# Scores and state @ w_in as groups of eight 64x32 matmuls, and softmax weights taken from VectorE block transposes

## The chip, the cores and the metric

The kernel runs on one core of one Trainium2 chip. The metric is the device time of one execution in microseconds (us). A core has a matrix engine (TensorE, called PE in the profile; its weight loads are the rows PEld), VectorE (DVE), ScalarE (ACT), GpSimd (POOL) and SyncE (SP), which here only issues DMAs. Each engine works through its own instructions in order and waits for the others by semaphores.

## What is computed

The reference is a cross attention between tokens `x` and a small recurrent state, followed by a feed-forward block. There are 8 batches, 8 heads, 512 tokens of 64 numbers per head, and 32 states per head; the feed-forward block goes from 512 to 2048 and back to 512. All is float32; the two weight matrices arrive as float64.

```python
# x: (8, 8, 512, 64)   state: (8, 8, 32, 64)
scores  = scale * x @ state^T          # 512 x 32 per head
a       = softmax(scores)              # over the 32 states
xread   = a @ state
scores2 = scale * state @ x^T          # 32 x 512 per head
a2      = softmax(scores2)             # over the 512 tokens
sread   = a2 @ x
y = concat([xread, sread])             # (8, 544 tokens, 512)
h = y @ w_in                           # 512 -> 2048
out = (h * sigmoid(1.702 * h)) @ w_out # 2048 -> 512
```

`scores2` is the transpose of `scores`; only the axis of the softmax differs.

## The kernel before

`xread @ w_in` is taken as `a @ M` with M = `state @ w_in` per head, so that the first product of a batch contracts over 8 heads x 32 states = 256 rows instead of 512. The work of one batch has two stretches:

- **Up** (`up`, matmuls at line 301, tiles `h`): for each of 16 blocks of 128 columns, two matmuls of M against the transposed softmax weights `aT`; ScalarE takes the sigmoid (L303), VectorE multiplies (L305, tiles `g`).
- **Down** (`down`, L317, tiles `o`): for each of 4 row blocks, 16 matmuls against `w_out`, cut into 4 quarters, so 16 slots of 4 matmuls in all. After each quarter comes one slot of the *next* batch's attention, from the table in `att_slots`: the transpose of the state (`att_state`, L158), the transposes of x (`att_xT`, L172), the scores and their softmaxes, the transposes of the softmax weights, and `att_sread` (L263). In eight of the slots one piece of M (`att_M`, L231) is added behind.

Before the change, the state of each pair of heads stands in a block-diagonal tile `sbd` (128 rows: 2 heads x 64; 128 columns: 4 heads x 32, zero outside the pair's two blocks; written by four VectorE copies at L162). Three things are multiplied with it on the whole 128x128 array:

- `att_x_scores` (L183, two calls a batch, tiles `s` with 64 columns): scores with tokens on the partitions, for the softmax over states (L193 to L201 on VectorE, the exponential at L196 on ScalarE);
- `att_s_scores` (L211, two calls, tiles `s` with 512 columns): the same scores with states on the partitions, for the softmax over tokens (L213 to L220, the exponential at L217);
- `att_M` (L231, eight calls, two matmuls each), evacuated by one VectorE or ScalarE copy (L233).

`att_aT` (L243) then transposes the first softmax's weights on TensorE and ScalarE copies them out (L244); `att_eT` (L253) does so for the second.

Batch 0 has nothing to hide behind: its attention, the rounding of `w_in` from float64 words (`round_weight`, four VectorE instructions and two GpSimd ones per tile, L122 to L130) and M run first, and the rounding of `w_out` runs inside batch 0's up. The loads are issued by SP in program order: state and x of batch 0 (L88, L91), then `w_in` through three buffers (L103). The order on PE, ACT, POOL and SP is the program's; that on VectorE is set by the framework's scheduler. PSUM tiles of the attention come from a pool of four banks (`psA`).

Of the kernel before, what the change touches and what calls it, by code (L numbers as in the profile page):

```python
# [20 lines left out]
def kernel(  # L21
# [24 lines left out]
    HG = P // Ns             # heads of a group: their states fill the partitions  # L46
    NG = H // HG             # groups of heads
    NPR = H // 2             # pairs of heads: 2 * D rows
# [4 lines left out]
    NFC = DF // FC  # L53
    scale = float(1.0 / np.sqrt(D))
    eps = 1e-9
    assert (2 * D, HG * Ns, NPR * P, DM, NFC) == (P, P, DM, FC, SCH)

    out_b = out.rearrange("(b t) n -> b t n", b=B)
    x_v = x.rearrange("b h (c q) d -> b c q h d", q=P)
# [23 lines left out]
    xn, stn = {}, {}  # L83

    def load(b):
        stn[b] = apool.tile([P, NG, 2, D], FP32, tag="stn", name=f"stn_{b}")
        for k in range(2):
            nc.sync.dma_start(stn[b][:, :, k, :], st_v[b])  # L88
        xn[b] = xpool.tile([P, SCH, H, D], FP32, tag="xn", name=f"xn_{b}")
        for c in range(SCH):  # L90
            nc.sync.dma_start(xn[b][:, c], x_v[b, c])  # L91

    def x_pair(b, c, p):
        return xn[b][:, c, 2 * p : 2 * p + 2].rearrange("q h d -> q (h d)")
# [3 lines left out]
    w_in_words, w_out_words = moe_w_in.bitcast(I32), moe_w_out.bitcast(I32)  # L98
    raw = {}

    def load_weight(key, src):
        raw[key] = wpool.tile([P, 2 * FC], I32, tag="raw", name="raw_" + "_".join(map(str, key)), bufs=3)
        nc.sync.dma_start(raw[key], src)  # L103

    def load_w_in(c):
        for k in range(NPR):
            load_weight(("i", c, k), w_in_words[P * k : P * (k + 1), 2 * FC * c : 2 * FC * (c + 1)])

    def load_w_out(f):
        load_weight(("o", f), w_out_words[P * f : P * (f + 1)])  # L110
# [15 lines left out]
        # the fraction's upper 20 bits below the leading 1, then its lower 32 in one rounding  # L126
# [16 lines left out]
    # block-diagonal state^T of each pair of heads, zero elsewhere; each batch  # L143
    # rewrites the same blocks
    sbd = [konst.tile([P, NPR, P], FP32, name=f"sbd_{i}") for i in range(2)]
    for t in sbd:
        nc.gpsimd.memset(t, 0.0)
    # sread^T of all batches: [d of a pair, pair, batch, n]
    srT = konst.tile([P, NPR, B, Ns], FP32, name="srT")

# [1 line left out]
    A = {}  # L152

    def att_state(b):
        A[b] = {"sbd": sbd[b % 2]}
        ps = att_ps([P, NG, P], f"stT_{b}")
        for g in range(NG):
            nc.tensor.transpose(ps[:, g], stn[b][:, g].rearrange("p k d -> p (k d)"), ident)  # L158
        for j in range(HG):
            r = slice(D * (j % 2), D * (j % 2) + D)  # L160
            cols = slice(Ns * j, Ns * (j + 1))
            nc.vector.tensor_copy(  # L162
                sbd[b % 2][r].rearrange("p (g k) c -> p g k c", g=NG)[:, :, j // 2, cols],
                ps[r, :, cols],
            )

    def att_xT(b, p):
        if p == 0:
            A[b]["xT"] = apool.tile([P, NPR, S], FP32, tag="xT", name=f"xT_{b}", bufs=1)
        ps = att_ps([P, SCH, P], f"xT_{b}_{p}")  # L170
        for c in range(SCH):
            nc.tensor.transpose(ps[:, c], x_pair(b, c, p), ident)  # L172
        dst = A[b]["xT"][:, p]
        (nc.scalar.copy if p % 2 else nc.vector.tensor_copy)(dst, ps.rearrange("p c q -> p (c q)"))  # L174

    def att_x_scores(b, i):
        # softmax of the x tokens over the states, two chunks of tokens at a time
        a = A[b]
        ps = att_ps([P, 2, NPR, 2 * Ns], f"s1_{b}_{i}")
        for c in range(2):  # L180
            for p in range(NPR):
                o = 2 * Ns * (p % (HG // 2))
                nc.tensor.matmul(  # L183
                    ps[:, c, p],
                    a["xT"][:, p, P * (2 * i + c) : P * (2 * i + c + 1)],
                    a["sbd"][:, p, o : o + 2 * Ns],
                    start=True,
                    stop=True,
                )
        sv = ps.rearrange("p c k (j n) -> p (c k j) n", n=Ns)  # L190
        n = 2 * H
        mx = apool.tile([P, n], FP32, tag="mx", name=f"mx_{b}_{i}")
        nc.vector.reduce_max(out=mx, in_=sv, axis=AX.X)  # L193
        e = apool.tile([P, n, Ns], FP32, tag="e1", name=f"e1_{b}_{i}")
        nc.vector.tensor_tensor(out=e, in0=sv, in1=mx.to_broadcast((P, n, Ns)), op=ALU.subtract)  # L195
        nc.scalar.activation(out=e, in_=e, func=AF.Exp, scale=scale)  # L196
        sm = apool.tile([P, n], FP32, tag="sm", name=f"sm_{b}_{i}")
        nc.vector.reduce_sum(out=sm, in_=e, axis=AX.X)
        nc.vector.tensor_scalar(sm, sm, eps, None, ALU.add)
        nc.vector.reciprocal(out=sm, in_=sm)  # L200
        nc.vector.tensor_tensor(out=e, in0=e, in1=sm.to_broadcast((P, n, Ns)), op=ALU.mult)  # L201
        a["e1", i] = e

    def att_s_scores(b, g):
        # softmax of the states over the x tokens
        a = A[b]
        ps = att_ps([P, S], f"s2_{b}_{g}")
        k = NPR // NG
        for i in range(k):
            p = k * g + i  # L210
            nc.tensor.matmul(ps, a["sbd"][:, p], a["xT"][:, p], start=(i == 0), stop=(i == k - 1))  # L211
        mx = apool.tile([P, 1], FP32, tag="mx2", name=f"mx2_{b}_{g}")
        nc.vector.tensor_reduce(out=mx, in_=ps, axis=AX.X, op=ALU.max, negate=True)  # L213
        nc.vector.tensor_scalar(mx, mx, scale, None, ALU.mult)
        e = apool.tile([P, S], FP32, tag="e2", name=f"e2_{b}_{g}")
        sm = apool.tile([P, 1], FP32, tag="sm2", name=f"sm2_{b}_{g}")
        nc.scalar.activation(out=e, in_=ps, func=AF.Exp, bias=mx, scale=scale, accum_out=sm)  # L217
        nc.vector.tensor_scalar(sm, sm, eps, None, ALU.add)
        nc.vector.reciprocal(out=sm, in_=sm)
        nc.vector.tensor_scalar(e, e, sm, None, ALU.mult)  # L220
        a["e2", g] = e

    def att_M(b, c, g):
        a = A[b]
        if c == 0 and g == 0:
            a["M"] = mpool.tile([P, NG, DF], FP32, tag="M", name=f"M_{b}")
        ps = att_ps([P, FC], f"M_{b}_{c}_{g}")
        k = NPR // NG
        for i in range(k):
            p = k * g + i  # L230
            nc.tensor.matmul(ps, a["sbd"][:, p], w_in[c][:, p], start=(i == 0), stop=(i == k - 1))  # L231
        dst = a["M"][:, g, FC * c : FC * (c + 1)]
        (nc.scalar.copy if g else nc.vector.tensor_copy)(dst, ps)  # L233

    def att_aT(b, g):
        # x-token weights: [states of a group, tokens]
        a = A[b]
        if g == 0:
            a["aT"] = apool.tile([P, NG, S], FP32, tag="aT", name=f"aT_{b}", bufs=1)
        ps = att_ps([P, SCH, P], f"aT_{b}_{g}")  # L240
        for c in range(SCH):
            e = a["e1", c // 2].rearrange("p (c g j) n -> p c g (j n)", c=2, g=NG)
            nc.tensor.transpose(ps[:, c], e[:, c % 2, g], ident)  # L243
        nc.scalar.copy(a["aT"][:, g], ps.rearrange("p c q -> p (c q)"))  # L244

    def att_eT(b, g):
        # state weights: [tokens of a chunk, states of a group]
# [4 lines left out]
        for c in range(SCH):  # L252
            nc.tensor.transpose(ps[:, c], a["e2", g][:, P * c : P * (c + 1)], ident)  # L253
        nc.vector.tensor_copy(a["eT"][:, g], ps)  # L254

    def att_sread(b):
        a = A[b]
        ps = att_ps([P, NPR, 2 * Ns], f"sr_{b}")
        k = NPR // NG
        for p in range(NPR):  # L260
            o = 2 * Ns * (p % k)
# [138 lines left out]
```

## Time and profile before

| | |
|---|---|
| runs (us) | 1029.76, 1025.52, 1028.1; median 1028.1 |
| span of the profiled execution | 1027.2 us (the page gives no other time for it) |
| busy: PE, PEld | 965.7 us (94%), 476.3 us (46%) |
| busy: DVE, ACT, POOL | 318.7 us (31%), 181.5 us (18%), 74.0 us (7%) |
| granted TensorE clock, mean | 0.970 of full speed |

The span runs from the first to the last instruction. "Busy" of PE is the union of its matmul records, whose ends are modelled; a float32 matmul leaves two records, each with its own weight load, and a transpose leaves one. A mean duration per record is longer than the distance between the starts of two records, since one begins before the one ahead of it has ended. "Idle before" is time in which the engine stood still ahead of an instruction, with what released it.

### The profile page before, as it was taken

What the parts mean: (1) busy time and instruction counts of PE and PEld (TensorE: products, weight loads), DVE (VectorE), ACT (ScalarE), POOL (GpSimd) and SP (SyncE); (2) the same over time, 40 slices, a digit from 0 to 9 for tenths busy, and PEclk for the clock granted to TensorE, in tenths of its full rate; (3) what the DMA queues carried; (4) which work ended last, traced back from release to release, by engine and by line L of the source; (5) the groups of instructions that cost most, each with busy time, mean ns of one, the idle gap of its engine ahead of it and who ended that gap; (6) DMA issues with size and microseconds to landing.
All of it is one profiled execution on the core that took longest, in us unless ns stands there. A gap on an engine that the chain in (4) does not pass through costs nothing.

```text
span 1027.2 us, 7083 instructions
## 1 busy us (share of the span) xinstructions
PE 965.7 (94%) x2832; PEld 476.3 (46%) x2832; DVE 318.7 (31%) x592; ACT 181.5 (18%) x306; POOL 74.0 (7%) x106
## 2 busy tenths in 40 slices
PE   4757599999999999999999999999999999999996
PEld 3512145454545454544545454545454454444662
DVE  5798953123221313031312231132303131210110
ACT  0102112122111311131212111121113111310110
POOL 3244420000000000000000000000000000000000
PEclk9558999999999999999999999999999999999998
DMA  6255430020002000020002000200000000000000
GB/s 173 67 161 161 157 89 11 10 52 5 11 11 61 1 16 10 15 48 16 11 10 52 5 11 10 62 1 10 11 21 0 11 11 11 11 10 11 20 1 21
DMA packets 45377, 35.59 MB, mean 35 GB/s; under 512 B 39072, under 2 KB 39072, under 8 KB 45344
## 3 DMA queue, kind: packets, MB, share of 16 engines
q1 hardware_dynamic: 42240, 26.22, 9.5%
q0 software_dynamic: 3104, 8.92, 2.2%
q8 instruction: 22, 0.36, 0.1%
q14 instruction: 11, 0.09, 0.0%
HBM read 26.21 MB, written 8.91 MB: 34 GB/s over the span
## 4 chain that ended last, share of the span: by engine, by line
issue 68%; PE 19%; DVE 9%; POOL 2%; DMA 1%; SPq 0%; ACT 0%; POOLq 0%
PE o L317 9%; PE M L231 3%; PE h L301 3%; POOL out_dram L323 1%; PE sr L263 1%; DVE fr_o L128 1%; DVE w_in L130 1%; DVE g L305 1%; DVE fr_i L128 1%; DVE sc_o L125 1%; DVE w_out L130 1%; DVE w_out L129 1%; PE s L183 1%; PE s L211 1%; DVE sc_i L125 1%
## 5 line engine op out<-in xcount | busy, mean ns | idle before, releaser
L317 PE MATMUL o<-w_out,g 128*128 128x512 f32 x1024 | 456.8, 592 | 0.0
L317 PEld LDWEIGHTS o<-w_out,g 128*128 128x128 f32 x1024 | 191.3, 190 | 224.8 <-issue 224.8
L301 PE MATMUL h<-aT,M 128*128 128x512 f32 x512 | 225.6, 597 | 19.0 <-DVE g L305 19.0
L301 PEld LDWEIGHTS h<-aT,M 128*128 128x128 f32 x512 | 91.6, 190 | 148.2 <-DVE g L305 81.6
L231 PE MATMUL M<-w_in,sbd 128*128 128x512 f32 x256 | 133.2, 643 | 13.9 <-DVE w_in L130 13.8
L305 DVE TENSOR_TENSOR g<-h,e 128x512 f32<-128x512 f32 x128 | 88.3, 690 | 122.7 <-ACT e L303 122.7
L303 ACT ACTIVATE e<-h 128x512 f32<-128x512 f32 x128 | 76.4, 597 | 180.8 <-PE h L301 180.8
L231 PEld LDWEIGHTS M<-w_in,sbd 128*128 128x128 f32 x256 | 47.6, 202 | 68.5 <-issue 48.5
L323 POOL DMA_DIRECT2D out_dram<-osb x32 | 17.6, 550 | 807.2 <-ACT osb L322 807.2
L322 ACT COPY osb<-o 128x512 f32<-128x512 f32 x32 | 18.8, 586 | 224.5 <-PE o L317 126.4
L254 DVE COPY eT<-eT 128x512 f32<-128x512 f32 x16 | 11.1, 691 | 130.2 <-PE eT L253 130.1
L233 DVE COPY M<-M 128x512 f32<-128x512 f32 x32 | 22.0, 688 | 84.6 <-PE M L231 84.6
L233 ACT COPY M<-M 128x512 f32<-128x512 f32 x32 | 18.6, 582 | 95.1 <-PE M L231 95.0
L183 PEld LDWEIGHTS s<-sbd,xT 128*128 128x128 f32 x256 | 31.7, 196 | 6.7 <-issue 6.7
L263 PEld LDWEIGHTS sr<-eT,xn 128*128 128x128 f32 x256 | 33.0, 209 | 3.8 <-issue 3.8
L263 PE MATMUL sr<-eT,xn 128*128 128x64 f32 x256 | 32.8, 292 | 0.1
L183 PE MATMUL s<-sbd,xT 128*128 128x64 f32 x256 | 30.9, 276 | 0.0
L305 DVE TENSOR_TENSOR g_sr<-h_sr,e_sr 128x256 f32<-128x256 f32 x16 | 6.8, 425 | 75.3 <-ACT e_sr L303 75.3
L211 PE MATMUL s<-xT,sbd 128*128 128x512 f32 x64 | 30.0, 593 | 0.0
L174 ACT COPY xT<-xT 128x512 f32<-128x512 f32 x16 | 9.4, 586 | 107.7 <-PE xT L172 107.7
L196 ACT ACTIVATE e<-e 128x512 f32<-128x512 f32 x16 | 10.1, 630 | 101.3 <-DVE e L195 101.3
L301 PE MATMUL h_sr<-srT,w_in 128*128 128x256 f32 x128 | 27.8, 379 | 0.0
(56 smaller groups left out, 474.3 us busy)
## 6 DMA issues: line engine op xcount, KB each, us to landing
xn<-in_x_dram SPq DMA_DIRECT2D x32, 256.0 KB, 4.4
raw_i<-in_moe_w_in_dram SPq DMA_DIRECT2D x16, 512.0 KB, 4.0
raw_o<-in_moe_w_out_dram SPq DMA_DIRECT2D x16, 512.0 KB, 3.3
out_dram<-osb POOLq DMA_DIRECT2D x32, 256.0 KB, 2.3
stn<-in_state_dram SPq DMA_DIRECT2D x16, 64.0 KB, 2.2
out_dram<-osb_sr POOLq DMA_DIRECT2D x2, 256.0 KB, 7.0
```

The lines of the kernel that those rows point to most:

```text
L125: nc.vector.scalar_tensor_tensor(sc, hi, -0x80000000, sc, ALU.bitwise_and, ALU.bitwise_or)
L128: nc.vector.tensor_scalar(fr, hi, 0xFFFFF, 0x100000, ALU.bitwise_and, ALU.bitwise_or)
L183: nc.tensor.matmul(ps[:, c, p], a["xT"][:, p, P * (2 * i + c) : P * (2 * i + c + 1)], a["sbd"][:, p, o : o + 2 * Ns], start=True, stop=True,)
L211: nc.tensor.matmul(ps, a["sbd"][:, p], a["xT"][:, p], start=(i == 0), stop=(i == k - 1))
L231: nc.tensor.matmul(ps, a["sbd"][:, p], w_in[c][:, p], start=(i == 0), stop=(i == k - 1))
L233: (nc.scalar.copy if g else nc.vector.tensor_copy)(dst, ps)
L263: nc.tensor.matmul(ps[:, p], x_pair(b, c, p), a["eT"][:, p // k, c, o : o + 2 * Ns], start=(c == 0), stop=(c == SCH - 1),)
L301: nc.tensor.matmul(hps, lhs[i], rhs[i], start=(i == 0), stop=(i == n - 1))
L303: nc.scalar.activation(out=e, in_=hps, func=AF.Sigmoid, scale=1.702)
L305: nc.vector.tensor_tensor(out=gt, in0=hps, in1=e, op=ALU.mult)
L317: nc.tensor.matmul(ops, G[key][f][:, P * r : P * (r + 1)], w_out[f], start=(f == 0), stop=(f == NF - 1))
L323: nc.gpsimd.dma_start(dst, osb)
```

## The change

- `sbd` goes. The state of a batch is transposed once into one tile `stT` of 128x128: 64 rows for heads 0 to 3, 64 rows for heads 4 to 7, and 32 columns for each head of a half.
- A new `by_state` replaces the matmuls of the scores and of M. It issues eight matmuls of 64 rows by 32 columns with 512 moving columns, one for each head. Each addresses its own part of the array: rows by the half g, columns by the head j in the half. The halves write different PSUM banks.
- The scores are computed once, states on the partitions (`att_scores`, slot 6). The softmax over tokens reads them as before. The softmax over states reads a copy made by VectorE's 32x32 block transpose (L196), all 1024 values per partition at once (`att_x_softmax`), and a second block transpose (L221) gives `aT`. `att_aT` with its TensorE transposes and ScalarE copies goes.
- `att_M` is called four times a batch, in slots 8 to 11, instead of eight times in slots 2 to 9.
- Heads are paired as j and j + 4 instead of neighbours, so x is loaded in eight DMAs a batch instead of four, each `w_in` tile in two DMAs of 64 rows instead of one of 128, and the state in one instead of two.

The core of the diff (new line numbers: `by_state` matmul L179, transposes of x L169, `up` L284, `down` L300):

```diff
     def load(b):
-        stn[b] = apool.tile([P, NG, 2, D], FP32, tag="stn", name=f"stn_{b}")
-        for k in range(2):
-            nc.sync.dma_start(stn[b][:, :, k, :], st_v[b])
+        stn[b] = apool.tile([P, NG, D], FP32, tag="stn", name=f"stn_{b}")
+        nc.sync.dma_start(stn[b], st_v[b])
...
         for c in range(SCH):
-            nc.sync.dma_start(xn[b][:, c], x_v[b, c])
+            for g in range(NG):
+                nc.sync.dma_start(xn[b][:, c, :, g], x_v[b, c, g])
...
     def load_weight(key, src):
-        nc.sync.dma_start(raw[key], src)
+        for i in range(src.shape[0]):
+            n = P // src.shape[0]
+            nc.sync.dma_start(raw[key][n * i : n * (i + 1)], src[i])
...
+    def by_state(b, rhs, name):
+        ps = [att_ps([P, FC], f"{name}_{g}") for g in range(NG)]
+        for j in range(NPR):
+            for g in range(NG):
+                rows, st = slice(D * g, D * (g + 1)), slice(Ns * j, Ns * (j + 1))
+                nc.tensor.matmul(ps[g][st], A[b]["stT"][rows, st], rhs(rows, j), start=True, stop=True)
+        return ps
+
+    def att_scores(b):
+        a = A[b]
+        ps = by_state(b, lambda rows, j: a["xT"][rows, j], f"s_{b}")
...
+            nc.scalar.activation(out=e, in_=ps[g], func=AF.Exp, bias=mx, scale=scale, accum_out=sm)
+            nc.vector.transpose(t[:, g].rearrange("p i n -> p (i n)"), ps[g])
...
+    def att_x_softmax(b):
+        a = A[b]
+        n = NG * NB
+        t = a["e1"].rearrange("p g i n -> p (g i) n")
...
+        nc.vector.transpose(
+            a["aT"].rearrange("p g t -> p (g t)"), a["e1"].rearrange("p g i n -> p (g i n)")
+        )
...
-    def att_M(b, c, g):
+    def att_M(b, c):
...
-        for i in range(k):
-            p = k * g + i
-            nc.tensor.matmul(ps, a["sbd"][:, p], w_in[c][:, p], start=(i == 0), stop=(i == k - 1))
+        ps = by_state(b, lambda rows, j: w_in[c][rows, j], f"M_{b}_{c}")
...
-            at(5 + i, att_x_scores, b, i)
-        for g in range(NG):
-            at(7 + g, att_s_scores, b, g)
-        for g in range(NG):
-            at(10 + g, att_aT, b, g)
+        at(6, att_scores, b)
+        at(6, att_s_softmax, b)
+        at(7, att_x_softmax, b)
...
-            if ahead and 2 <= u < 2 + NFC * NG:
-                att_M(b + 1, *divmod(u - 2, NG))
+            if ahead and 8 <= u < 8 + NFC:
+                att_M(b + 1, u - 8)
```

What moves on the engines is seen in three places. In the rows, `o` is the output of down, `w_out` and `g` its operands; numbers behind a name are counters of tiles, and x8 stands for eight matmuls in a row.

**PE, down of batch 0, around slots 5 and 6.** Before, each quarter of down is followed by score matmuls and a piece of M:

```order
L317 MATMUL o_1_827<-w_out_106,g_7_626 128x512
L183 MATMUL s_1_0_846<-sbd_116,xT_788 128x64 x8
L231 MATMUL M_1_1_865<-w_in_96,sbd_116 128x512 x2
L317 MATMUL o_1_827<-w_out_107,g_8_644 128x512
...
L183 MATMUL s_1_1_873<-sbd_116,xT_788 128x64 x8
L231 MATMUL M_2_0_892<-w_in_97,sbd_116 128x512 x2
L317 MATMUL o_1_827<-w_out_111,g_12_716 128x512
```

and now by one group of eight small matmuls, first for the scores and from the ninth quarter on for M (the pair of rows comes four times in each group):

```order
L300 MATMUL o_1_813<-w_out_110,g_11_696 128x512
L179 MATMUL s_0_832<-xT_783,stT_777 32x512
L179 MATMUL s_1_833<-xT_783,stT_777 32x512
...
L300 MATMUL o_1_813<-w_out_111,g_12_714 128x512
...
L300 MATMUL o_2_881<-w_out_102,g_3_552 128x512
L179 MATMUL M_0_0_887<-w_in_95,stT_777 32x512
L179 MATMUL M_0_1_888<-w_in_95,stT_777 32x512
```

The score and M matmuls of the whole array have become five groups of eight, each between two matmuls of down.

**DVE, the same stretch.** Before, the softmax over states goes through two half-sized chains:

```order
L195 TENSOR_TENSOR e_1_0_857<-s_1_0_846,mx_0_855 128x512
L198 TENSOR_REDUCE sm_0_860<-e_1_0_857 128x16
L199 TENSOR_SCALAR sm_0_860<-sm_0_860 128x16
L200 RECIPROCAL sm_0_860<-sm_0_860 128x16
L201 TENSOR_TENSOR e_1_0_857<-e_1_0_857,sm_0_860 128x512
L193 TENSOR_REDUCE mx_1_882<-s_1_1_873 128x16
L195 TENSOR_TENSOR e_1_1_884<-s_1_1_873,mx_1_882 128x512
L233 COPY M_805<-M_2_0_892 128x512
```

and now through one chain of double width that begins and ends with block transposes:

```order
L196 STREAM_TRANSPOSE e_1_842<-s_1_833 128x512
...
L212 TENSOR_REDUCE mx_870<-e_1_842 128x32
...
L213 TENSOR_TENSOR e_1_842<-e_1_842,mx_870 128x1024
...
L231 COPY M_886<-M_0_0_887 128x512
L216 TENSOR_REDUCE sm_874<-e_1_842 128x32
L217 TENSOR_SCALAR sm_874<-sm_874 128x32
L218 RECIPROCAL sm_874<-sm_874 128x32
L219 TENSOR_TENSOR e_1_842<-e_1_842,sm_874 128x1024
L221 STREAM_TRANSPOSE aT_879<-e_1_842 128x1024
L231 COPY M_886<-M_1_0_903 128x512
```

The first copy of M stands ahead of the sum of the softmax, the second behind the whole chain.

**PE, the attention of batch 0, at the start of the program.** Before:

```order
L211 MATMUL s_0_1_254<-xT_179,sbd_115 128x512 x2
L243 MATMUL aT_0_267<-ident,e_0_0_215 128x128 x2
...
L253 MATMUL eT_0_280<-ident,e_0_0_248 128x128 x4
L253 MATMUL eT_1_286<-ident,e_0_1_260 128x128 x4
L263 MATMUL sr_292<-eT_279,xn_123 128x64 x16
L231 MATMUL M_0_0_312<-w_in_95,sbd_115 128x512 x2
L231 MATMUL M_0_1_316<-w_in_95,sbd_115 128x512 x2
```

and now:

```order
L179 MATMUL s_1_205<-xT_179,stT_177 32x512
L240 MATMUL eT_0_247<-ident,e_0_0_218 128x128 x4
L240 MATMUL eT_1_253<-ident,e_0_1_225 128x128 x4
L248 MATMUL sr_259<-eT_246,xn_118 128x64 x16
L179 MATMUL M_0_0_279<-w_in_95,stT_177 32x512
L179 MATMUL M_0_1_280<-w_in_95,stT_177 32x512
```

The transposes for `aT` no longer stand between the scores and those for `eT`, and both halves of M need all four tiles of a `w_in` chunk.

## Rows read from the trace of the kernel before

**Rows 1.** The page: busy tenths and granted clock in 40 slices of the span
```profile
PE   4757599999999999999999999999999999999996
...
DVE  5798953123221313031312231132303131210110
...
PEclk9558999999999999999999999999999999999998
```

**Rows 2.** Windows: length; busy us of PE, PEld, DVE, ACT, POOL; clock, DMA share, GB/s
```profile
244.26:354.70 110.44, 110.44 (x331) 53.86 (x330) 27.48 (x52) 21.76 (x36) 2.17 (x4) 1.00 0.08 21
...
0.00:133.81 133.81, 82.37 (x202) 38.52 (x203) 112.82 (x201) 18.93 (x31) 51.94 (x69) 0.80 0.47 146
```

**Rows 3.** Timeline of PE, one batch: start us, us, engine line op tiles xcount
```profile
247.69 0.38 PE L158 MATMUL stT<-ident,stn 128*128 128x128 f32 x2
247.91 3.60 PE L317 MATMUL o<-w_out,g 128*128 128x512 f32 x8
...
255.65 1.88 PE L231 MATMUL M<-w_in,sbd 128*128 128x512 f32 x4
257.37 3.60 PE L317 MATMUL o<-w_out,g 128*128 128x512 f32 x8
...
271.98 1.90 PE L183 MATMUL s<-sbd,xT 128*128 128x64 f32 x16
273.71 1.94 PE L231 MATMUL M<-w_in,sbd 128*128 128x512 f32 x4
...
285.86 1.88 PE L211 MATMUL s<-xT,sbd 128*128 128x512 f32 x4
287.57 1.88 PE L231 MATMUL M<-w_in,sbd 128*128 128x512 f32 x4
...
304.74 0.60 PE L243 MATMUL aT<-ident,e 128*128 128x128 f32 x4
305.18 3.60 PE L317 MATMUL o<-w_out,g 128*128 128x512 f32 x8
...
327.18 27.68 PE L301 MATMUL h<-aT,M 128*128 128x512 f32 x64
354.70 3.60 PE L317 MATMUL o<-w_out,g 128*128 128x512 f32 x8
```

**Rows 4.** Groups of PE, the same batch: xcount | busy us, mean ns | idle before
```profile
L317 PE MATMUL o<-w_out,g 128*128 128x512 f32 x128 | 57.4, 592 | 0.0
...
L231 PE MATMUL M<-w_in,sbd 128*128 128x512 f32 x32 | 15.2, 596 | 0.0
```

**Rows 5.** Timeline of PEld: weight loads, the idle time before each in brackets
```profile
300.45 0.19 PEld L231 LDWEIGHTS M<-w_in,sbd 128*128 128x128 f32 x1 [0.24 <-issue]
...
304.74 0.36 PEld L243 LDWEIGHTS aT<-ident,e 128*128 128x128 f32 x3 [0.29 <-issue]
```

**Rows 6.** Groups of DVE, the same batch
```profile
L201 DVE TENSOR_TENSOR e<-e,sm 128x512 f32<-128x512 f32 x2 | 1.4, 692 | 0.1
...
L254 DVE COPY eT<-eT 128x512 f32<-128x512 f32 x2 | 1.4, 692 | 18.6 <-PE eT L253 18.6
...
L162 DVE COPY sbd<-stT 64x64 f32<-64x64 f32 x4 | 0.9, 222 | 2.4 <-PE stT L158 2.3
```

**Rows 7.** Timeline of PE, start of the program
```profile
11.51 4.41 PE L183 MATMUL s<-sbd,xT 128*128 128x64 f32 x32
15.76 3.65 PE L211 MATMUL s<-xT,sbd 128*128 128x512 f32 x8
30.49 0.66 PE L243 MATMUL aT<-ident,e 128*128 128x128 f32 x2 [11.08 <-DVE sm L218]
...
81.30 2.07 PE L231 MATMUL M<-w_in,sbd 128*128 128x512 f32 x2 [1.15 <-DVE w_in L130]
...
90.09 1.98 PE L301 MATMUL h<-aT,M 128*128 128x512 f32 x4 [0.87 <-DVE g L305]
```

**Rows 8.** Timeline of SP's queue, start of the program
```profile
1.74 3.22 SPq L91 DMA_DIRECT2D xn<-in_x_dram  x4
```

More of the change, by code (lines that the diff above doesn't have):

```diff
@@ L154, in att_state @@
     def att_state(b):
-        A[b] = {"sbd": sbd[b % 2]}
-        ps = att_ps([P, NG, P], f"stT_{b}")
-        for g in range(NG):
[L158 to L176, printed above, removed]
-        a = A[b]
[L179 to L198, printed above, removed]
@@ new lines, in att_state, with att_xT @@
+        A[b] = {}
+        ps = att_ps([P, P], f"stT_{b}")
+        nc.tensor.transpose(ps, stn[b].rearrange("p g d -> p (g d)"), ident)
+        A[b]["stT"] = apool.tile([P, P], FP32, tag="stT", name=f"stT_{b}")
+        nc.vector.tensor_copy(A[b]["stT"], ps)
+    def att_xT(b, j):
+        if j == 0:
+            A[b]["xT"] = apool.tile([P, NPR, S], FP32, tag="xT", name=f"xT_{b}", bufs=1)
+        ps = att_ps([P, SCH, P], f"xT_{b}_{j}")
+        for c in range(SCH):
+            nc.tensor.transpose(ps[:, c], x_heads(b, c, j), ident)
+        dst = A[b]["xT"][:, j]
+        (nc.scalar.copy if j % 2 else nc.vector.tensor_copy)(dst, ps.rearrange("p c q -> p (c q)"))
@@ L223, in att_M @@
-    def att_M(b, c, g):
-        a = A[b]
-        if c == 0 and g == 0:
-            a["M"] = mpool.tile([P, NG, DF], FP32, tag="M", name=f"M_{b}")
[L227 to L230, printed above, removed]
-            nc.tensor.matmul(ps, a["sbd"][:, p], w_in[c][:, p], start=(i == 0), stop=(i == k - 1))
[L232 to L244, printed above, removed]
+        nc.vector.tensor_tensor(out=t, in0=t, in1=sm.to_broadcast((P, n, Ns)), op=ALU.mult)
@@ new lines, in att_x_softmax @@
+        a["aT"] = apool.tile([P, NG, S], FP32, tag="aT", name=f"aT_{b}", bufs=1)
+        nc.vector.transpose(
+            a["aT"].rearrange("p g t -> p (g t)"), a["e1"].rearrange("p g i n -> p (g i n)")
+        )
+    def att_M(b, c):
+        a = A[b]
+        if c == 0:
+            a["M"] = mpool.tile([P, NG, DF], FP32, tag="M", name=f"M_{b}")
+        ps = by_state(b, lambda rows, j: w_in[c][rows, j], f"M_{b}_{c}")
+        for g in range(NG):
+            (nc.scalar.copy if g else nc.vector.tensor_copy)(a["M"][:, g, FC * c : FC * (c + 1)], ps[g])
@@ L257, in att_sread @@
         a = A[b]
[L258 to L261, printed above, removed]
+        ps = att_ps([P, NPR, NG, Ns], f"sr_{b}")
+        for j in range(NPR):
             for c in range(SCH):
                 nc.tensor.matmul(
-                    ps[:, p],
-                    x_pair(b, c, p),
-                    a["eT"][:, p // k, c, o : o + 2 * Ns],
+                    ps[:, j],
+                    x_heads(b, c, j),
+                    a["eT"][:, :, c, Ns * j : Ns * (j + 1)],
                     start=(c == 0),
@@ L269, in att_sread @@
                 )
-        for j in range(2):
-            r = slice(D * j, D * (j + 1))
-            nc.vector.tensor_copy(srT[r, :, b, :], ps[r, :, Ns * j : Ns * (j + 1)])
+        for g in range(NG):
+            r = slice(D * g, D * (g + 1))
+            nc.vector.tensor_copy(srT[r, :, b, :], ps[r, :, g, :])
     def att_slots(b):
@@ L368 @@
         for i in range(4):
-            down("sr", r, i, out_b[nb * r : nb * (r + 1), S:ST, :])
+            down("sr", r, i, out_s[nb * r : nb * (r + 1)])
 _INS = ['x', 'state', 'moe_w_in', 'moe_w_out']
```

74 lines of the change are left out of this document (38 added, 36 removed).

## The prediction

> **What bounds the kernel now.** I read the page's 40 slices first. PE shows 9 in every slice from the sixth on, while DVE swings between 0 and 3 there; before that DVE has the 9s and PE has gaps [rows 1]. So there are two stages with different limits. The windows put numbers on them: in the start, up to 133.81 us, DVE is busy 112.8 us and PE 82.4 us; in one later batch of 110.44 us PE is busy all 110.44 us and DVE 27.5 us [rows 2]. [...] In the batches the time is therefore the sum of what PE does, and I take it from the timeline of PE, from the start of one piece to the start of the next: the modelled duration of a record is 592 ns [rows 4], but the 64 records of up take 354.70 - 327.18 = 27.52 us, so the pitch of a full matmul record is 0.43 us [rows 3], and the eight records of a quarter of down take 3.44 us. A batch has 16 matmuls of M and 32 records [rows 4]: a float32 matmul is two records, 0.86 us. The weight load of a record takes 0.19 us and lies under the matmul ahead, with 0.24 us to spare [rows 5].
>
> **The change, part by part.** Seven batches (1 to 7) have their attention inside the down of the batch before. There PE loses, per batch:
>
> - M: eight pieces, each 257.37 - 255.65 = 1.72 us [rows 3]: 13.76 us
> - scores for the softmax over states: two pieces of 273.71 - 271.98 = 1.73 us: 3.46 us
> - scores for the softmax over tokens: two pieces of 287.57 - 285.86 = 1.72 us: 3.44 us
> - transposes for `aT`: two pieces of 305.18 - 304.74 = 0.44 us: 0.88 us
> - one of two state transposes: half of 247.91 - 247.69 = 0.22 us: 0.11 us
>
> Together 21.65 us. It gains five groups of eight small matmuls (one of scores, four of M). If a group costs C, the balance per batch is 5C - 21.65 us, and the **break-even is C = 4.33 us**.
>
> C is the unknown of this case: no row shows a matmul on a part of the array. A group is 8 matmuls of 512 columns, so 16 records. Streaming 512 float32 columns costs a record 0.43 us however few rows and columns of weights it has, I take it, since only the moving side sets it. From below: every part runs by itself, and the two records of a matmul follow each other, 0.86 us. From above: nothing overlaps, 16 x 0.43 = 6.88 us. In all rows PE's matmuls start in the order of the program, and the two records of one matmul need the same part of the array. So I let the second record of a matmul wait 0.43 us for the first; the next matmul, on another part, starts only behind it, together with it. That overlaps pairs and no more: 8 x 0.43 + 0.43 = 3.87 us. Coming back to the whole array, the last part has to run out: 592 - 430 = 162 ns [rows 3, 4], once per group. **C = 4.03 us**, between the ends and nearest to the only order that the rows show.
>
> [...]
>
> So 5 x 4.03 = 20.15 us come for 21.65 us: -1.50 us a batch, **-10.5 us** in seven.
>
> What else is touched in the batches, I cost at nothing while PE is full. VectorE gets two block transposes of 512 and one of 1024 elements per partition, bounded by the 0.69 us of a 512-element copy or product [rows 6] and twice that (my estimate of the upper end, since it writes across partitions): 2.8 to 5.5 us, less 0.9 us for the four `sbd` copies. On 27.5 of 110.44 us [rows 2] that is covered. Behind it queues the second copy of M, which now stands after the sum, product and transpose of the softmax: about 3 x 1.38 + 0.6 = 4.7 us late at worst. Its bank is wanted again two groups later, 2 x (3.44 + C) away, so 14.9 us; at the shortest C it is still 8.6 us. The transposes for the other weights come four slots later. ScalarE loses the two `aT` copies. The eight x loads instead of four go out a batch ahead.
>
> **The start** is VectorE's. There the added 2.8 us of transposes less 0.9 us of copies lie on the path: about +2 us. Each x load takes 3.22 / 4 = 0.8 us of SP's queue ahead of the first `w_in` load [rows 8]; eight of half the size cost as much together, or up to 3.2 us more if a DMA's cost does not depend on its size. The last matmul of M there took 2.07 us for its two records [rows 7], twice the pace of a batch and with the clock low [rows 1]; four records that overlap in pairs end up to 1.7 us later. Against that, the `aT` pieces no longer stand ahead of the other transposes: two records took 0.66 us, so all eight some 2.6 us, behind an 11.08 us wait for DVE [rows 7]. The scores took 11.51 to 15.76 us and 3.65 us more there; whatever of that goes only lengthens the wait. Sum: **+2 us**, ends -3 and +7 us. Up of batch 0 waits for DVE in each of its blocks (`g` in the row of 90.09) [rows 7], and the last stretch, with no attention in it, stays as it is.
>
> Against the profiled span: 1027.2 - 10.5 + 2 = 1018.7 us. The median of the runs is 0.9 us above that span, so the forecast is **1020 us**. Its own range: C from 3.44 us (the halves of the array each run their four heads in line, 8 x 0.43) to 4.57 us (0.16 us drain and a bare 0.19 us weight load on both sides) gives -31 to +8 us; with the start, 994 to 1043 us.
>
> **The rivals.**
>
> *All eight parts run at once.* For it: the eight matmuls share no weights, no output rows of one bank, and each pair could queue at its own part. Against: the first record of the second matmul would have to start before the second record of the first matmul has had its turn. Then C is 0.86 us plus what it takes to hand out the records: between nothing and 0.11 us per load and matmul, which is what a transpose costs (four in 0.44 us) [rows 3], so 16 x 0.11 + 0.43 = 2.2 us at most. With C = 1.5 us in the middle: 7.5 - 21.65 = -14.15 us a batch, -99 us in seven; 929 us, ends 907 and 954. PE stays full: slots of 3.44 + 1.5 us still hold VectorE's 29 to 32 us a batch. [...]
>
> *Nothing overlaps (slower).* PE takes the small matmuls one by one, because the second record's weights must wait for the first, or because parts that share columns or rows conflict on the stream. The place is the same five groups; C = 16 x 0.43 + 0.16 = 7.04 us. 35.2 - 21.65 = +13.55 us a batch, +95 us in seven, +4 us in the start: **1127 us**. It decides from C = 4.33 us on, only 0.3 us above my forecast. For it: a chunk of M now streams through eight matmuls instead of four, so without overlap the time of M doubles. Against: each matmul of a group has rows and columns of the array to itself, and the halves alternate.
>
> **How the numbers follow.** A measurement of this kernel can tell about 0.5% (5 us) from no change. I give the forecast 0.47, full overlap 0.38, no overlap 0.15. In the forecast's case the sum lies 8 us below the median, and 0.14 us of C is worth 5 us: of its 0.47 I count 0.25 as faster, 0.14 as within 0.5% and 0.08 as slower. Faster: 0.25 + 0.38 = 0.63; same 0.14; slower 0.08 + 0.15 = 0.23. The range of 915 to 1040 us leaves out the case without overlap (0.15) and the outer ends of the two others (about 0.05). Full overlap is so far from the forecast that the range has a thin middle.
>
> **What would show it.** In the timeline of PE, from the first record of a group (L179) to the next record of down (L300): 4.0 us with starts 0.43 us apart in pairs is my case; 1 to 2 us is the first rival, about 7 us the second. The period of a batch should be 108.9 us, against 96 or 124 us. In the start, up of batch 0 should still wait for `g`, and the first record of down come near 136 us instead of 133.8. I am wrong in the mechanism if C leaves 3.4 to 4.6 us, and wrong in the cover if PE shows idle time between slots 7 and 15 with DVE as its releaser.

## The result: 931.4 us, and the profile after

| | before | changed |
|---|---|---|
| median of 4 runs on one chip (us) | 1028.93 | 931.4 (929.3 to 931.92) |
| ratio of the times | | 0.9054, 95% interval [0.9036, 0.9071] |
| span of the profiled execution (its time 931.92) | 1027.2 | 930.2 |
| busy PE, PEld | 965.7, 476.3 | 850.7, 384.4 |
| busy DVE, ACT | 318.7, 181.5 | 320.3, 169.7 |
| mean granted clock | 0.970 | 0.948 |

The page's slices answer to [rows 1]. There are still two stages: a start in which DVE has the high digits and PE has gaps, and batches in which PE stands at 9. PE's 9s begin in the eighth slice instead of the sixth, although a slice has become shorter.

```profile
PE   3545568999999999999999999999999999999995
...
DVE  5786896413232223322232314231523141300110
...
PEclk8555799999999999999999999999999999999998
```

The windows, with the columns of [rows 2]: the start up to the first record of down, and one batch.

```profile
0.00:146.22 146.22, 76.86 (x202) 27.67 (x203) 113.55 (x195) 17.65 (x28) 51.47 (x67) 0.70 0.48 133
...
241.02:335.83 94.81, 94.81 (x331) 42.30 (x330) 27.60 (x46) 20.26 (x33) 2.16 (x4) 1.00 0.08 23
```

These two rows hold the whole result. A batch went from 110.44 to 94.80 us (from 146.22 over 241.02 to 335.83), -15.64 us, and seven of them make -109.5 us. The start went from 133.81 to 146.22 us, +12.4 us. Together that is -97.1 us, and the spans differ by 97.0 us. What is left of the span, from the down of batch 7 on, is the same: 1027.2 - (133.81 + 7 x 110.44) = 120.3 us before, 930.2 - (146.22 + 7 x 94.80) = 120.4 us now. So there was a larger gain than I forecast, and a loss that I had mostly not seen.

The timeline of PE, with the columns of [rows 3, 7]. First two rows at the end of the start, then the groups of scores and M in the down of batch 1:

```profile
89.53 8.74 PE L284 MATMUL h<-aT,M 128*128 128x512 f32 x16
...
144.40 1.98 PE L284 MATMUL h<-aT,M 128*128 128x512 f32 x4 [1.50 <-DVE g L288]
146.22 3.60 PE L300 MATMUL o<-w_out,g 128*128 128x512 f32 x8
...
267.02 1.09 PE L179 MATMUL s<-xT,stT 64*32 64x512 f32 x16
268.04 7.13 PE L300 MATMUL o<-w_out,g 128*128 128x512 f32 x16
275.10 1.09 PE L179 MATMUL M<-w_in,stT 64*32 64x512 f32 x16
276.12 3.70 PE L300 MATMUL o<-w_out,g 128*128 128x512 f32 x8
279.75 1.09 PE L179 MATMUL M<-w_in,stT 64*32 64x512 f32 x16
```

A group of sixteen records is busy for 1.09 us. What it costs is read from start to start: 279.75 - 275.10 = 4.65 us for a group and a quarter of down; the quarter alone takes 3.43 us, the 3.44 us of [rows 3]. So **C = 1.22 us** for all eight matmuls, the changeover (what it costs to go from the whole array to its parts and back) included. From the first record of the group to the next of down, the sign that the prediction named, it is 276.12 - 275.10 = 1.02 us.

### The profile page after: what moved, and what is told of

The parts are those of the page before. It is cut to its first block, busy times and chain, and to the rows that moved or that the text cites. A ratio compares the mean times of both kernels' runs of the same rounds, so it can differ in the third digit from the quotient of the medians.

```text
span 930.2 us, 7058 instructions
## 1 busy us (share of the span) xinstructions
PE 850.7 (91%) x2824; PEld 384.4 (41%) x2824; DVE 320.3 (34%) x544; ACT 169.7 (18%) x282; POOL 73.5 (8%) x104
## 4 chain that ended last, share of the span: by engine, by line
issue 67%; PE 18%; DVE 9%; POOL 4%; SPq 0%; DMA 0%; ACT 0%; POOLq 0%
PE o L300 11%; PE h L284 4%; POOL out_dram L306 2%; PE M L179 1%; PE sr L248 1%; DVE sc_i L133 1%; POOL sc_i L132 1%; DVE w_out L138 1%; DVE fr_o L136 1%; DVE w_out L137 1%; POOL sc_i L131 1%; DVE sc_o L133 1%; DVE w_in L138 1%; DVE g L288 1%; PE xT L169 1%
## 5 line engine op out<-in xcount | busy, mean ns | idle before, releaser
L300 PE MATMUL o<-w_out,g 128*128 128x512 f32 x1024 | 457.8, 596 | 0.0
L300 PEld LDWEIGHTS o<-w_out,g 128*128 128x128 f32 x1024 | 187.8, 190 | 236.1 <-issue 236.1
L284 PE MATMUL h<-aT,M 128*128 128x512 f32 x512 | 229.3, 606 | 21.4 <-DVE g L288 21.4
L284 PEld LDWEIGHTS h<-aT,M 128*128 128x128 f32 x512 | 92.9, 193 | 153.1 <-DVE g L288 83.4
L179 PE MATMUL M<-w_in,stT 64*32 64x512 f32 x512 | 55.5, 658 | 26.0 <-DVE w_in L138 25.9
L171 DVE COPY xT<-xT 128x512 f32<-128x512 f32 x16 | 11.1, 692 | 77.4 <-PE xT L169 77.4
L191 DVE TENSOR_REDUCE mx<-s 128x1 f32<-128x512 f32 x16 | 10.4, 687 | 79.1 <-PE s L179 79.1
L179 PEld LDWEIGHTS M<-w_in,stT 64*32 64x32 f32 x512 | 7.6, 108 | 68.1 <-issue 38.2
L257 DVE COPY srT<-sr 64x128 f32<-64x128 f32 x16 | 4.6, 289 | 73.0 <-PE sr L248 72.9
L284 PE MATMUL h_sr<-srT,w_in 128*128 128x256 f32 x128 | 27.8, 379 | 0.0
L300 PE MATMUL o_sr<-w_out,g_sr 128*128 128x512 f32 x64 | 27.6, 592 | 0.0
```

Of the source, the lines that this page charges most:

```text
L171: (nc.scalar.copy if j % 2 else nc.vector.tensor_copy)(dst, ps.rearrange("p c q -> p (c q)"))
L179: nc.tensor.matmul(ps[g][st], A[b]["stT"][rows, st], rhs(rows, j), start=True, stop=True)
L284: nc.tensor.matmul(hps, lhs[i], rhs[i], start=(i == 0), stop=(i == n - 1))
L300: nc.tensor.matmul(ops, G[key][f][:, P * r : P * (r + 1)], w_out[f], start=(f == 0), stop=(f == NF - 1))
```

## The experiments

They answer two questions: what rule gives C = 1.22 us, and where the 12.4 us of the start come from. None of the kernels leaves work out.

The theories on C are models of mine, and the runs measure the times that they give: **Q**, each part of the array has a line of its own, and only records of the same part wait for each other. **L**, the records go in the program's order, and PE looks past one waiting record but not two. **P**, my forecast: no looking past. On the start: **V**, the longer softmax chain on VectorE accounts for the 12 us. **W**, it comes from `w_in` and M: two DMAs to a tile, M wanting all four tiles of a chunk before its first copy, and VectorE's order.

### e1_pairs and e2_two: two chunks of M in one group

A part gets two matmuls instead of one, so four records need it one after the other. In e1 the two stand side by side in the program; in e2 all eight parts come once, then all eight again. The diff is that of e1; in e2 the loop over `i` is the outermost.

```diff
+    def att_M2(b, c):
...
+        for j in range(NPR):
+            for g in range(NG):
+                for i in range(2):
...
+                    nc.tensor.matmul(
+                        ps[i][g][st], a["stT"][rows, st], w_in[c + i][rows, j], start=True, stop=True
+                    )
...
-            if ahead and 8 <= u < 8 + NFC:
-                att_M(b + 1, u - 8)
+            if ahead and u in (9, 11):
+                att_M2(b + 1, u - 9)
```

> The changed kernel, but in batches 1 to 7 M is made of two chunks of w_in at a time: each part of the array gets the matmuls of both chunks, four records in a row, before the program goes to the next part. Theory Q (each part of the array has its own line of records, and only records of the same part wait for each other): a group of 32 records lasts 4 x 0.43 + 0.36 = 2.1 us against 2 x 1.22 us for two groups of the changed kernel; 0.3 us less, 14 groups, 4 us less: 927 us. Theory L (the matrix engine starts records in the program's order and looks past one waiting record only, just enough for the two records of one matmul): the third record of a part holds up all others, each part takes 2 x 0.43 us before the next comes on, a group lasts 7.7 us, 14 x 5.3 us more: 1005 us. Theory P (the forecast, no look-ahead at all) gives 14 us for a group: about 1090 us.

> The same two chunks at a time and the same PSUM banks as the run before, but all eight parts get the first chunk's matmul before any gets the second's. It is the control for the order: by theory Q both last 2.1 us a group and the two kernels agree within 2 us (927 us); by theory L this one is at 927 to 932 us and the other about 75 us above it.

Measured: e1 925.65 us, ratio 0.9008 [0.8979, 0.9038]; e2 925.98 us, 0.901 [0.8984, 0.9035]. The timelines of PE, e1 first:

```profile
275.35 1.99 PE L243 MATMUL M<-w_in,stT 64*32 64x512 f32 x32
277.27 7.13 PE L318 MATMUL o<-w_out,g 128*128 128x512 f32 x16
284.33 1.99 PE L243 MATMUL M<-w_in,stT 64*32 64x512 f32 x32
```

```profile
277.84 1.95 PE L243 MATMUL M<-w_in,stT 64*32 64x512 f32 x32
279.72 7.13 PE L318 MATMUL o<-w_out,g 128*128 128x512 f32 x16
286.79 1.95 PE L243 MATMUL M<-w_in,stT 64*32 64x512 f32 x32
```

From the group's first record to the next of down it takes 1.92 us in e1 and 1.88 us in e2. The windows of the first group of e1 (length; busy us of PE and of PEld, with their records, of this line alone; clock, DMA share, GB/s) show that eight matmul records are in work within the first 0.12 us and that it is still only eight until 275.76:

```profile
275.34:275.46 0.12, 0.11 (x8) 0.12 (x15) 1.00 0.00 0
275.46:275.76 0.30, 0.30 (x8) 0.11 (x15) 1.00 0.00 0
275.82:275.92 0.10, 0.10 (x16) 0.10 (x8) 1.00 0.00 0
```

So for some 0.4 us no ninth record starts. In the program the second matmul of a part stands directly behind its first and needs the same rows and columns. Had the program's order held between parts, all matmuls behind it would have waited with it: by the expectation 7.7 us a group (L) or 14 us (P), where 1.92 us was measured. L and P fall; of the three, Q with its 2.1 us is the one that fits. By what means PE picks its next record no run shows. The order of the matmuls is worth 0.04 us a group, 1.92 against 1.88 us, and the medians differ by 0.3 us; where the 0.04 us lie was not shown, nor whether the two records of one matmul start next to each other. A merged group costs 284.33 - 275.35 = 8.98 less 16 x 0.43 = 2.10 us, against 2 x 1.22 = 2.44 us for two, so a changeover costs 0.34 us; 14 of them saved are 4.8 us, and the medians fell by 5.8 and 5.4 us. In e1 part of that lies in the start (down began at 143.66 us, in e2 at 146.25 us), which the theories on C do not speak of.

### e3_halves: two parts instead of eight

The same eight matmuls, but each loads 64 rows by all 128 columns, zero outside its head's 32, and the four of a half add into one bank. So the halves still lie side by side, and the four heads of a half follow each other.

```diff
...
-                rows, st = slice(D * g, D * (g + 1)), slice(Ns * j, Ns * (j + 1))
-                nc.tensor.matmul(ps[g][st], A[b]["stT"][rows, st], rhs(rows, j), start=True, stop=True)
+                rows = slice(D * g, D * (g + 1))
+                nc.tensor.matmul(
+                    ps[g], A[b]["sbd"][rows, j], rhs(rows, j), start=(j == 0), stop=(j == NPR - 1)
+                )
```

> The changed kernel with the same eight matmuls in each group, but each on a whole half of the array: 64 rows by 128 columns, with weights that are zero outside the head's 32 columns. Four matmuls then share a part. If the gain comes from parts that run side by side (theory Q): the four matmuls of a half go in line, 8 records x 0.43 = 3.44 us plus 0.3 us of changing over, 3.75 us a group against 1.22: 35 groups x 2.53 = 89 us more, 1020 us. If it came only from fewer columns of weights or from shorter loads, with the two halves not side by side, a group would last 6.9 us: about 1130 us. If column parts did not matter at all: 931 us.

Measured 1018.57 us, ratio 0.9911 [0.9885, 0.9937]. The timeline of PE:

```profile
286.00 3.70 PE L184 MATMUL M<-w_in,sbd 64*128 64x512 f32 x16
289.64 3.70 PE L307 MATMUL o<-w_out,g 128*128 128x512 f32 x8
293.27 1.99 PE L184 MATMUL M<-w_in,sbd 64*128 64x512 f32 x8
```

293.27 - 286.00 = 7.27 us less 3.43 us gives C = 3.84 us: 8 records of 0.43 us one after the other in each half, 3.44 us, and 0.40 us for the changeover. Two records of the group are in work at a time (windows 286.00:286.10 and 286.10:286.40, x2 in both). Splitting the columns as well is what makes most of the gain; the halves alone would have given the time that I forecast, by another mechanism. (35 groups at 2.62 us more are 92 us, and the medians differ by 87 us: the start of e3 ends at 141.43 us, 4.8 us earlier than that of the changed kernel, which no run looked into.)

### e4_soft: the other half of the change alone

The kernel before, with its block-diagonal matmuls and its eight pieces of M; only the softmax over states now works on block transposes of the state scores, and the score matmuls with 64 columns and the TensorE transposes for `aT` go. (The diff is against the kernel before.)

```diff
-    def att_x_scores(b, i):
...
+    def att_scores(b):
...
+            nc.vector.transpose(t[:, g].rearrange("p i n -> p (i n)"), ps)
...
-    def att_aT(b, g):
...
-            at(5 + i, att_x_scores, b, i)
...
+        at(6, att_scores, b)
+        at(6, att_s_softmax, b)
+        at(7, att_x_softmax, b)
```

> The kernel before with one part of the change alone: the scores once, and the softmax over states on block transposes; the scores and M stay on the whole array with block-diagonal weights, the layout of heads, x and w_in stays too. In batches 1 to 7 the second scores (3.46 us) and the transposes for aT (0.88 us) go: 4.34 x 7 = 30 us less. For the start, which became 12 us longer with the change, theory V (the longer softmax chain on VectorE) expects the 12 us here as well: 1010 us. Theory W (w_in and M: two DMAs for each tile, all four tiles of a chunk before its first copy, and the order of VectorE that comes of it) expects a start within 3 us of the kernel before: 999 us.

Measured 1000.48 us, ratio 0.9731 [0.9704, 0.9757]. The timeline of PE:

```profile
136.23 3.60 PE L303 MATMUL o<-w_out,g 128*128 128x512 f32 x8
139.67 0.38 PE L158 MATMUL stT<-ident,stn 128*128 128x128 f32 x2
...
245.66 0.38 PE L158 MATMUL stT<-ident,stn 128*128 128x128 f32 x2
```

A batch takes 245.66 - 139.67 = 105.99 us, 4.45 us less than before; the 3.46 us of scores and 0.88 us of `aT` transposes that go are 4.34 us. The start ends at 136.23 us, +2.4 us. So V is out: the softmax chain costs 2.4 us here, and the other 10 of the 12.4 us come with what e4 does not have, above all the split loads and M in groups.

### e5_neigh, e6_act, e7_late: three edits in the start

The waits of DVE in the start say where to look (us in total, times, longest): the kernel before up to 133.81 us, then the changed one up to 146.22 us.

```profile
DVE g L305 <- ACT e L303: 2.4, 1, 2.4
DVE sc_i L125 <- POOL sc_i L124: 2.0, 4, 0.5
DVE M L233 <- PE M L231: 1.6, 1, 1.6
```

```profile
DVE M L231 <- PE M L179: 5.7, 3, 2.0
...
DVE sc_i L133 <- POOL sc_i L132: 4.6, 9, 0.5
DVE g L288 <- ACT e L286: 4.5, 2, 3.5
```

DVE does as much as before, 113.55 against 112.82 us [rows 2], but stands still for 146.22 - 113.55 = 32.7 us instead of 21.0 us. Of these 11.7 us more, the three waits shown make 8.8 us (14.8 instead of 6.0 us). A copy of M has to wait for matmuls that want all four tiles of a chunk, where a piece of M wanted two. The rounding of `w_in` waits nine times instead of four for GpSimd's part of the same tile. And where up begins, the timeline of DVE shows two products `g` ahead of the first rounding of `w_out` in VectorE's order, so that it idles for 3.47 and 1.02 us with all of `w_out` still to round:

```profile
86.93 0.69 DVE L138 SCALAR_TENSOR_TENSOR w_in<-w_in,sc_i 128x512 f32<-128x512 f32 x1
89.63 0.69 DVE L231 COPY M<-M 128x512 f32<-128x512 f32 x1 [2.00 <-PE M L179]
93.78 0.69 DVE L288 TENSOR_TENSOR g<-h,e 128x512 f32<-128x512 f32 x1 [3.47 <-ACT e L286]
95.50 0.69 DVE L288 TENSOR_TENSOR g<-h,e 128x512 f32<-128x512 f32 x1 [1.02 <-ACT e L286]
96.11 0.42 DVE L130 TENSOR_SCALAR sc_o<-raw_o 128x512 int32<-128x512 int32 x1
```

The wait of 3.47 us is not one for a load of `w_out`: the first was issued at 82.81 us (timeline of SP's queue), and none of `w_out` took more than 5.0 us to land (view of the tile `raw_o`), so the words lay there by 87.8 us, ahead of the end of that copy of M at 90.3 us.

e5 pairs neighbouring heads again, so that x and `w_in` come in one DMA to a chunk and tile:

```diff
-    x_v = x.rearrange("b (g j) (c q) d -> b c g q j d", g=NG, c=SCH)
...
+    x_v = x.rearrange("b h (c q) d -> b c q h d", c=SCH)
...
-            load_weight(("i", c, k), w_in_rows[k, :, :, 2 * FC * c : 2 * FC * (c + 1)])
+            load_weight(("i", c, k), w_in_words[P * k : P * (k + 1), 2 * FC * c : 2 * FC * (c + 1)])
```

e6 gives ScalarE all M copies of batch 0, e7 issues the loads of batch 1 only behind the third `w_out` tile:

```diff
-            (nc.scalar.copy if g else nc.vector.tensor_copy)(a["M"][:, g, FC * c : FC * (c + 1)], ps[g])
+            (nc.scalar.copy if g or b == 0 else nc.vector.tensor_copy)(a["M"][:, g, FC * c : FC * (c + 1)], ps[g])
```

```diff
-    load(1)
     for b in range(B):
...
             if b == 0:
+                if f == 3:
+                    load(1)
                 load_w_out(f)
```

> The changed kernel with heads paired as neighbours again: x in four DMAs a batch, each w_in tile in one DMA; the state takes four small DMAs. Everything on the array stays. If the split DMAs are behind the longer start (146.2 us to the first matmul of down, against 133.8 before): 6 to 12 us less, 919 to 925 us. If not: within 2 us of 931 us.

> The changed kernel with both copies of M on ScalarE in batch 0, none on VectorE. If VectorE's wait for the last of four w_in tiles at the head of its queue (three waits, 5.7 us in all, and four copies of 0.69 us) is on the path of the start: 6 to 8 us less, 923 to 925 us. If the start is set by loads or GpSimd instead: no change.

> The changed kernel with the loads of batch 1 issued inside the up of batch 0, behind the third load of w_out instead of ahead of the first. VectorE's order then has the first rounding of w_out ahead of the first products g, where the changed kernel has two products first and VectorE stands still for 5.5 us. If that is on the path: 5 us less, 926 us. If the products are late for another reason: no change.

| | median (us) | ratio [95%] | down begins (us) | against 146.22 | DVE waits for M, GpSimd on `w_in`, `g` (us) |
|---|---|---|---|---|---|
| before | 1028.93 | | 133.81 | -12.4 | 1.6, 2.0, 2.4 |
| changed | 931.4 | 0.9054 [0.9036, 0.9071] | 146.22 | | 5.7, 4.6, 4.5 |
| e5_neigh | 927.27 | 0.9016 [0.8998, 0.9035] | 141.64 | -4.6 | 4.8, 1.5, 3.2 |
| e6_act | 926.69 | 0.9007 [0.8988, 0.9025] | 141.27 | -5.0 | 0, 5.1, 7.2 |
| e7_late | 924.77 | 0.899 [0.8972, 0.9008] | 138.15 | -8.1 | 4.1, 4.6, 0 |

The last column is from the view of DVE's waits up to the time at which down begins. Each edit gives something, and each takes away most of one wait: e5 that for GpSimd, e6 that for M, e7 that for `g`. e5 and e6 stay below the 6 us that were expected of each. In e7 the timeline of DVE has the first rounding of `w_out` ahead of the last copy of M, and `g` comes without a wait:

```profile
84.91 0.42 DVE L130 TENSOR_SCALAR sc_o<-raw_o 128x512 int32<-128x512 int32 x1
...
87.93 0.69 DVE L231 COPY M<-M 128x512 f32<-128x512 f32 x1 [1.25 <-PE M L179]
...
92.78 0.68 DVE L288 TENSOR_TENSOR g<-h,e 128x512 f32<-128x512 f32 x1
```

e7 does two things at once, however: the loads of batch 1, which in the changed kernel take SP's queue from 77.24 to 82.71 us, no longer stand ahead of the first load of `w_out` (timeline of SP's queue), and no run separates an earlier load from the other order.

The three gains add up to 17.6 us, more than the 12.4 us that were lost. In e6, DVE's wait for `g` even grew to 7.2 us in all, so that some of the wait for M only moved behind it.

### e8_all and e9_best: the three edits together, then with e1's groups

e8 is the changed kernel with the three diffs of e5, e6 and e7, e9 is e8 with the diff of e1 (here a batch's two groups of 32 records).

> The three changes of the start together. If they add up and the start comes back to the 133.8 us of the kernel before: 12 us less, 919 us. If they remove the same wait: 5 to 8 us less, 923 to 926 us.

> The three changes of the start (heads paired as neighbours, both copies of M on ScalarE in batch 0, the loads of batch 1 later) together with M in groups of two chunks in batches 1 to 7. The start stays at 133.5 us to the first matmul of down; each pair of groups becomes one, 0.34 us less, fourteen times. By theory Q the two gains add: 919.4 - 4.8 = 914.6 us. If the longer groups hold up a copy or a bank in the batches: 919 us or more.

e8 took 919.42 us, ratio 0.8939 [0.8922, 0.8957]; e9 915.25 us, 0.892 [0.8894, 0.8946].

The window of the start of e8, up to its first record of down, with the columns of the windows above:

```profile
0.00:133.46 133.46, 75.24 (x201) 27.50 (x202) 113.27 (x191) 19.60 (x32) 51.44 (x67) 0.71 0.47 144
```

Down begins at 133.46 us, 0.3 us earlier than in the kernel before, and DVE stands still for 133.46 - 113.27 = 20.2 us, as before (21.0). Together the three edits give back 12.8 us, less than the 17.6 us of the single runs: they overlap, as an idle time that one edit fills is not there for the next. The three waits fall from 14.8 to 3.3 us (M none, GpSimd 1.5, `g` 1.8), which is 11.5 of the 12.5 us that DVE stands still for less. So the runs show that the start can be brought back almost by these waits alone. They do not show that the whole loss lay there: 3.3 us is less than the 6.0 us of the kernel before, so the edits also pay for the 2.4 us of the softmax chain, and only e5 takes back something that the change had brought; e6 and e7 do what neither kernel did. e9, with the merged groups, is 16.2 us faster than the changed kernel and the fastest version of this study (it ran on another chip than e8, where the kernel before took 1027.54 us instead of 1028.74 us); in its start down begins at 134.44 us, 1.0 us later than in e8, and its 14 saved changeovers outweigh that.

## Why the prediction was right or wrong

Faster, which had 0.63, was right; the forecast of 1020 us was not, by 89 us. The mechanism is that of the first rival, with all eight parts at once: the batch took 94.8 us (96 us there) and a group 1 to 2 us. That the time, too, came within 3 us of its 929 us is luck. The rival took C = 1.5 us and so -99 us in seven batches, where -109.5 us was measured, and its sum leaves out the +2 us of the start (with it 931 us), where +12.4 us was measured; the two misses of some 10 us cancel.

**The step that failed is the price C of a group.** "The next matmul, on another part, starts only behind it, together with it": from this came 8 x 0.43 + 0.43 + 0.16 = 4.03 us. It measured 1.22 us, and five times the difference of 2.81 us is 14.1 us a batch, 98 us in seven. That is most of the 89 us: the batches together gave -109.5 instead of -10.5 us, and the start took back 10.4 us of the difference. The windows of the group of M at 275.10 us show what happens instead (this line's records of PE and PEld alone):

```profile
275.06:275.16 0.10, 0.06 (x8) 0.06 (x14) 1.00 0.00 0
...
275.36:275.46 0.10, 0.10 (x8) 0.00 (x0) 1.00 0.00 0
275.46:275.56 0.10, 0.10 (x10) 0.00 (x0) 1.00 0.00 0
275.56:275.66 0.10, 0.10 (x16) 0.00 (x0) 1.00 0.00 0
```

By 275.16, 0.06 us behind the first start, eight records are in work and fourteen of the sixteen weight loads have begun. No further matmul record starts until the slice from 275.46 on, and by 275.66 all sixteen have. The second eight come some 0.45 us behind the first (x8 still in the window 275.52:275.54, x16 in 275.58:275.60). I read them as the first and the second record of each part: the first of all eight parts side by side, and no part held up by the waiting second record of another. I had reasoned from rows in which every matmul used the whole array and started 0.43 us behind the one ahead; these cannot tell an order of the whole program from an order within each part. e1 and e2 show the same with four records to a part (1.92 and 1.88 us a group), and in e3, where four matmuls do share a part, C is 3.84 us.

The rest of the sum by its steps:

- **What a batch loses, 21.65 us.** With 5 x 1.22 = 6.10 us the balance is -15.55 us; measured -15.64 us. e4, which takes the scores and `aT` away alone, gave 4.45 us for 4.34 us. The terms taken from the timeline of [rows 3] were right.
- **The 0.43 us of a small record**, an assumption for which no row of a small matmul stood, fit: two more records on each part cost 2.10 - 1.22 = 0.88 us in e1, 0.44 us each, where a record with the weights of the whole array took 0.43 us. Half the moving columns took half the time in the kernel before: its 128 records of `h_sr` (128x256) stand from 961.87 to the start of `o_sr` at 989.50 us, 0.22 us each (timeline of PE).
- **The break-even of 4.33 us** was right as a formula, and the forecast lay only 0.30 us below it. So the sign hung on a term for which I had bounds only. The bounds of C, 0.86 to 6.88 us, held the measured value.
- **The changeover.** I had put 0.16 us on one side of a group. Merging two groups shows 0.34 us, and the timeline says where it lies. The first record of down behind a group is followed by its second after 276.65 - 276.12 = 0.53 us instead of 0.43 us, 0.10 us late, and its weight load did not lie under a matmul ahead (timeline of PEld, below). Ahead of the group, 275.10 - (268.04 + 16 x 0.43) = 0.18 us pass, 0.10 us of them that same delay in the stretch before, so 0.08 us. Behind it, 276.12 - (275.10 + 0.06 + 2 x 0.43) = 0.10 us, where 0.06 us is the time within which the first eight records started (window 275.06:275.16):

```profile
275.10 0.18 PEld L179 LDWEIGHTS M<-w_in,stT 64*32 64x32 f32 x16 [0.76 <-issue]
276.12 0.30 PEld L300 LDWEIGHTS o<-w_out,g 128*128 128x128 f32 x2 [0.84 <-issue]
276.65 0.19 PEld L300 LDWEIGHTS o<-w_out,g 128*128 128x128 f32 x1 [0.24 <-issue]
```

In [rows 5] a weight load lies under the matmul ahead with 0.24 us to spare; here no load of down begins before 276.12, where its matmul begins too. A changeover costs about a third of a microsecond here, the 0.34 us of the merged groups. That PE drains at it, which the upper end of my range counted with 0.16 us on both sides of a group, no run shows; what the rows show is the 0.08, 0.10 and 0.10 us above.

- **The cover in the batches** held: PE has no idle time in them, and VectorE's busy time of 27.60 us is the 27.48 us of [rows 2] to 0.1 us. The block transposes cost what the lower bound said, 0.71 us for 512 elements and 1.25 us for 1024, 2.7 us a batch, and the VectorE work that went (the `sbd` copies, and two half-sized chains for one) paid for them:

```profile
L196 DVE STREAM_TRANSPOSE e<-s 128x512 f32<-128x512 f32 x16 | 11.1, 714 | 14.4 <-ACT e L195 14.4
...
L221 DVE STREAM_TRANSPOSE aT<-e 128x1024 f32<-128x1024 f32 x8 | 10.0, 1246 | 0.3
L219 DVE TENSOR_TENSOR e<-e,sm 128x1024 f32<-128x1024 f32 x8 | 9.8, 1223 | 0.2
```

- **The start, +2 us with ends -3 and +7**, was wrong at +12.4 us. The term that I gave (VectorE's transposes less its copies) measured 2.4 us in e4. What I left out is the order on VectorE. I had counted its busy time, which hardly changed, and took the waits of batch 0's up as they were; but there a late M copy, a late GpSimd step and two early `g` each add idle time, 8.8 us of the 11.7 us that DVE stood still for more. The x loads took 4.30 us of SP's queue instead of the 3.22 us of [rows 8], within the bound. PE's lower clock there (0.70 against 0.80 in the windows) has a share that no run separates. At the end of the start PE waits for `g` (the row of 144.40 us), but DVE's waits for M and most of its wait for the first `g` lie where the granted clock was 0.50 of full speed, as it was in the kernel before from 54 to 80 us. The rows are a window, with the columns of [rows 2], and the last four records behind a chunk of `w_in`, which took 1.92 us where the sixteen of a group in a batch took 1.09 us.

```profile
80.00:90.00 10.00, 6.16 (x13) 1.03 (x14) 6.84 (x12) 0.33 (x1) 3.32 (x4) 0.50 1.09 261
```

```profile
87.68 1.92 PE L179 MATMUL M<-w_in,stT 64*32 64x512 f32 x4 [1.70 <-DVE w_in L138]
```

So up to 0.8 us of each of the three waits for M may be the clock's (an estimate from these rows). e8 got back to 133.46 us at a mean clock of 0.71, so a higher clock was not needed for it.

- **The last stretch** stayed as it was, to 0.1 us.

## What to carry to other kernels

Small matmuls that each have rows and columns of the array to themselves cost here (eight of 64x32, 512 columns, float32) together what one of them costs, plus about a third of a microsecond for the changeover: 1.22 us, where the two records of one are 0.86 us. So put as many of them as the PSUM tiles allow into one group (two groups in one saved 0.34 us), and split columns as well as rows (3.84 us with rows alone, e3). Rows of one kind of instruction cannot tell in what order another kind starts: where a term decides the sign and only its bounds are known, the two ends are two cases, and the middle is none. In a stage whose bound engine has idle time, count what it waits for, in the order in which its instructions stand, and not its busy time alone.

## What was not expected of the hardware

- Eight first records on eight parts start within some 0.06 us, and sixteen weight loads of 64x32 take 0.18 us together (the row of 275.10 above), where one load of 128x128 takes 0.19 us [rows 5].
- A matmul that waits for its part did not hold up those of other parts behind it in the program: with four records to a part a group takes 1.92 us with the two matmuls of a part side by side in the program (e1) and 1.88 us with those of all other parts between them (e2), where waiting in the program's order would have made 7.7 us or more by the expectation of e1. So what is said at the head, that each engine works through its own instructions in order, did not hold here for PE between its parts.
- VectorE's block transpose costs about as much as a product of the same size: 1.25 against 1.22 us for 1024 elements, although it writes across partitions.
